# Sign bit by VectorE, a direct split of weights, pooling placed by the plan, and a plan that scores by age of readiness

## The chip, the cores and the metric

The kernel runs on one core of a Trainium2 chip. The metric is the device time of the whole program in microseconds. The engines are named as the profile names them: PE (matmul) with PEld (its weight loads), DVE (VectorE), ACT (ScalarE), POOL (GpSimd) and SP (which here only issues DMAs). Each engine has its own queue and executes it in order: an instruction whose input isn't there yet holds everything behind it on that engine.

## What is computed

Three layers over 4608 tokens of 512 features. The inputs `q`, `k`, `v` are float32; the four weights and the gain `g_ln` arrive as float64, which on the chip are pairs of 32-bit words, a low word and a high word.

```python
k_p = k.reshape(B, H, 72, 8, 64).mean(axis=3)        # pooling by 8, the same for v
attn = softmax(q @ k_p.T / 8);  x = attn @ v_p        # 8 batches, 8 heads, 576 queries, 72 keys
h = x @ w_in                                          # 512 -> 1024
solu = h * softmax(h)
ln = (solu - mean) / sqrt(var + 1e-6) * g_ln
y = ln @ w_out                                        # 1024 -> 512
h = y @ w2_in                                         # 512 -> 2048
out = (h * sigmoid(1.702 * h)) @ w2_out               # 2048 -> 512
```

## The kernel before

**Two stages.** The first stage does attention and the first two-layer block, tile by tile (36 tiles of 128 tokens, in 18 pairs), and beside it turns `w2_in` and `w2_out` into what the second stage multiplies with. The second stage runs 12 blocks of 384 tokens through `w2_in` and `w2_out` in a seven-product scheme; its order is written out by hand and no line of it is touched here.

**Numbers in two halves.** A float32 value is held as two float16 values, `hi` and `lo`, and a product is three matmul passes. `lo` is the value minus `hi`.

**From float64 to float32.** A piece of 512 columns of a weight (tile `raw`) is joined from its words: ACT writes the sign (`sg`), ACT shifts the low word down, ACT scales the high word (this drops the exponent's excess), DVE (`scalar_tensor_tensor`, shift and or) puts the two together into the low word's place, and POOL multiplies by `sg`. For the first layer `joined` (L646 on) does it; for the second layer `values_of` (L590 on), whose POOL product goes to the tile `w_f`.

**Split of the first layer's weights.** `first_half` (L645 on) handles the 16 pieces of `w_in` and `w_out`: ACT scales the joined piece into `val` (float32, two buffers that it shares with `w_f`), ACT rounds `val` to `hi`, and a subtraction on POOL or DVE (`VG`, the plan's choice) makes `lo`.

**The second layer's weights.** `Quarter.run` takes the 16 chunks of 1024 columns, each two pieces through `values_of`, four sums of slots (`combine`), `hi` on ACT and `lo` by `VG`, and two DMAs to a scratch in HBM.

**Attention of a tile** (`attention(t)`): load `qt`; matmul `psx` (one buffer); on DVE the largest `mx` and the difference `e`; ACT exp; DVE sum `rs`; the product `e<-e,rs` by `VG`; ACT and `VG` split into `st`; an SP transpose `aT<-st`; matmul `psv` (one buffer); ACT and DVE evict it as `xT` (hi and lo). **Hidden layer** (`Pair.hidden`): 24 matmuls into `psh` (two buffers), DVE `hmx` and `nm`, ACT exp `he`, DVE `tt` with the mean, ACT squares. **Norm and projection**: small POOL operations, ACT `tt` and `zs`, `zs` lo by `VG`, an SP transpose `zT`, 96 matmuls into `psy` (one buffer, two rounds), ACT `y`, store.

**Pooling** (`half`, L758 on): keys and values of a batch are loaded in two halves each (`half`, three buffers), 32 in all. A half is summed by one DVE `tensor_reduce`, or by three POOL adds (`total`). Before, the dictionary `KV_POOL` sends two of the 32 to POOL: keys of batch 0, second half, and values of batch 1, second half.

**What sets the order.** The first stage is emitted by a planner that runs on the host as the kernel is built (`Plan`, L171 on). Each step of work is a generator (a strand) that offers its next operation. `estimate` gives an operation a start time in a model of the engines: the later of the engine's free time and of the operation's inputs being ready; an operation with a choice of engines (`VG`) takes the one where it ends first, with 3000 ns held against DVE. `run` then emits the strand with the least score, which is that time plus up to 900 ns either way for how far its tile's due time lies from now (doubled in the first 60 us of the model). So the model's time, and not what happens on the chip, fixes the order of every queue; `there(...)` is an entry for no engine, with which a strand waits in the model's time until a tile is there.

Of the kernel before, what the change touches and what calls it, by code (L numbers as in the profile page):

```python
# [18 lines left out]
P = 128  # L19
# [18 lines left out]
UW = 256  # L38
# [30 lines left out]
DUE_MAX_IN = -10000  # L69
DUE_MAX_OUT = 20000  # L70

RAWS = 4
SG = 4
TTS = 4
V_TOP = 2.0 ** 14

TOP3 = 2.0 ** -29 * (1 - 2.0 ** -23)
A_TOP = 2.0 ** 14
LN_UP = 2.0 ** 10
CI_LEAST, CI_MOST = 2.0 ** -50, 2.0 ** 40  # L80
# [91 lines left out]
class Plan:  # L172
# [30 lines left out]
    def drop(self, *tiles):  # L203
        for t in tiles:
            del self.ring_of[t.name]
# [12 lines left out]
    def estimate(self, op):  # L218
        best = None
        for engine in op.engines:  # L220
            t = max(self.free[engine], self.ready(op, engine))
            if engine == "sp":
                t = max(t, self.free["dma"] - 2000)
            if engine == "dve" and op.port and self.pool_from <= t < self.free["pool"]:
                t = self.free["pool"]
            key = t + op.cost[engine] + self.spare[engine] if len(op.engines) > 1 else t
            if best is None or key < best[0]:
                best = (key, t, engine)
        return best[1:]

    def take(self, op, t, engine):
# [25 lines left out]
    def run(self):  # L257
        while self.strands:
            self.strands.sort(key=lambda s: s.due)
            while any([s.settle() for s in self.strands]):  # L260
                self.strands = [s for s in self.strands if not s.ended]
            best = None
            for s in self.strands:
                if isinstance(s.item, Op):
                    t, engine = self.estimate(s.item)
                    slack = (s.due - (t if self.now is None else self.now)) * self.haste
                    score = t + max(-self.pull, min(self.pull, slack)) * (self.early if t < self.until else 1)
                    if best is None or score < best[0]:
                        best = (score, t, engine, s)
            if best is None:  # L270
                assert not self.strands, "strands wait for each other"
                break
            _, t, engine, s = best
            s.item.emit(engine)
            self.take(s.item, t, engine)
            s.advance(None)
            self.strands = [s for s in self.strands if not s.ended]
# [3 lines left out]
def moe_kernel(ctx: ExitStack, tc: tile.TileContext, qT, kT, vT, w_in, w_out, g_ln, w2_in, w2_out, eye, outT):  # L281
# [135 lines left out]
    with ExitStack() as ph:  # L417
# [75 lines left out]
        def G(name, *args, **kw):  # L493
            return op(("pool",), name, args, kw)

        def VG(name, *args, **kw):
            return op(("pool", "dve"), name, args, kw)

        def A(**kw):
            return op(("act",), "activation", (), kw)  # L500
# [89 lines left out]
        def values_of(raw, up, dst, begun=None):  # L590

            hw, lw = raw[:, :, 1], raw[:, :, 0]
            sg = yield New(kv, [P, WC], F16, "sg", bufs=SG)
            if begun is not None:
                begun.append(sg)
            yield A(out=sg, in_=hw.bitcast(F32), func=AF.Sign)
            yield A(out=lw.bitcast(U32), in_=lw.bitcast(U32), func=AF.Copy, scale=TOP3, bias=-0.49999)
            yield lambda: (up.name, up.offset) in upped
            yield A(out=hw.bitcast(F32), in_=hw.bitcast(F32), func=AF.Copy, scale=up)
            yield V(  # L600
                "scalar_tensor_tensor", out=lw, in0=hw, scalar=3, in1=lw, op0=ALU.logical_shift_left,
                op1=ALU.bitwise_or,
            )
            d = yield from dst()
            yield G("tensor_tensor", out=d, in0=sg, in1=lw.bitcast(F32), op=ALU.mult)
            drop(sg)

        def raw_new(q, n):
            return New(kv, [P, q, n, 2], I32, "raw", "raw", RAWS)
# [35 lines left out]
        def first_half(raw, measured, scaled, up, k, c, his):  # L645

            yield from joined(raw, measured)
            yield scaled
            val = yield New(kv, [P, NS, UW], F32, "val", "w_f", 2)
            v = val.rearrange("p s f -> p (s f)")[:, :WC]  # L650
            hi, lo = (x[:, k, c] for x in his)
            yield A(out=v, in_=raw[:, :, 0].bitcast(F32), func=AF.Copy, scale=up)
            yield A(out=hi, in_=v, func=AF.Copy)
            yield VG("tensor_tensor", out=lo, in0=v, in1=hi, op=ALU.subtract)
            drop(val)

        def halves(n):
            return [slice(j * WC, (j + 1) * WC) for j in range(n // WC)]
# [73 lines left out]
            scaled = start(scale(), due)  # L732
            yield until(*[start(part(i), due + 4 * i) for i in range(n)])

        KV_POOL = {("k", 0): 1, ("v", 1): 1}

        def spans(t):

# [19 lines left out]
        def half(kind, b, j, src, dst):  # L758

            raw = yield New(kv, [P, 2, SP, NPOOL], F32, "half", bufs=3)  # L760
            begun[kind][b] += 1
            yield D(raw.rearrange("p a s o -> p a (s o)"), src[b][:, 2 * j : 2 * j + 2])
            yield from total(G if KV_POOL.get((kind, b)) == j else V, dst[:, 2 * j : 2 * j + 2], raw)
            drop(raw)

        def pooled(kind, b, src, due):
# [413 lines left out]
        def eye_load():  # L1180
            yield D(eye_t, eye)

        plan.early, plan.until = PULL_EARLY, EARLY_END
        plan.pull, plan.haste, plan.spare = PULL, HASTE, {"pool": 0.0, "dve": SPARE}

# [294 lines left out]
```

## Time and profile before

| | us |
|---|---|
| Median of three runs (lowest, highest) | 1255.61 (1253.86, 1258.69) |
| The profiled execution | 1253.29 |
| its span, first to last instruction | 1251.5 |
| PE busy | 1143.5 (91%) |
| DVE busy | 730.9 (58%) |
| ACT busy | 766.5 (61%) |
| POOL busy | 664.7 (53%) |

The profiled execution has 1.8 us around its span and lies 2.3 us under the median. The page gives shares over the whole span; since the two stages have different limits, the rows that follow are taken by stretches. A row of a group of instructions shows its line, engine and operation, output and inputs by name, shapes and number, then the total busy time and the mean length of one in ns, then the engine's idle time just before these instructions and what ended it. Line 475 and line 512 are the helpers through which the planner emits everything, so the names of the tiles tell the instructions apart.

### The profile page before, as it was taken

To read this page: it belongs to the slowest core of one execution; us is meant where nothing else is said; L and a number is where in the kernel's file an instruction comes from. 1 tells how busy PE (TensorE), PEld (TensorE's weight loads), DVE (VectorE), ACT (ScalarE), POOL (GpSimd) and SP (SyncE) were. 2 spreads that over 40 slices of the span, in tenths; PEclk is the share of its full clock that TensorE was granted. 3 is DMA by queue.
4 is the path that set the end of the run, shared out by engine and by line. 5 is a ranking of instruction groups with operands and counts; after the bars stand their busy time and mean duration, and the time that the engine had idled before them with its cause. 6 is when DMAs were issued, how large, how long until landed. Compare 5 with 4: busy or idle time off the path is not lost.

```text
span 1251.5 us, 27586 instructions
## 1 busy us (share of the span) xinstructions
PE 1143.5 (91%) x11678; PEld 989.6 (79%) x11678; DVE 730.9 (58%) x1153; ACT 766.5 (61%) x1073; POOL 664.7 (53%) x696
## 2 busy tenths in 40 slices
PE   2778998899999999889999999999999999999998
PEld 2335665576666666789999999999999898999998
DVE  7898877587677843136455454637272737364543
ACT  6998998788789855345445353627263536454552
POOL 5887998687879953424333352525262515243331
PEclk9989999899999999999999999999999999999999
DMA  9979999999989698470101010100011010101000
GB/s 324 302 205 240 269 270 256 248 231 248 256 206 234 164 230 236 109 270 8 46 14 39 14 40 20 33 27 27 27 33 46 7 46 8 46 7 46 14 14 26
DMA packets 246524, 152.85 MB, mean 122 GB/s; under 512 B 163584, under 2 KB 226176, under 8 KB 244096
## 3 DMA queue, kind: packets, MB, share of 16 engines
q1 hardware_dynamic: 246400, 151.09, 45.5%
q8 instruction: 91, 1.49, 0.5%
q14 instruction: 33, 0.27, 0.1%
HBM read 77.66 MB, written 33.55 MB: 89 GB/s over the span
## 4 chain that ended last, share of the span: by engine, by line
PE 30%; POOL 12%; DVE 8%; ACT 8%; issue 5%; DMA 0%; ACTq 0%; POOLq 0%
PE bank_a L1290 18%; PE bank_d L1290 8%; ACT w_g L1325 6%; DVE g L1337 5%; POOL w_g L336 3%; PE bank_b L1290 3%; POOL w_g L335 3%; POOL w_g L333 2%; POOL w_g L334 2%; PE psy L512 2%; ACT g L1334 1%; DVE c L1303 1%; POOL zs L475 1%; DVE w_g L333 0%; ACT c L1300 0%
## 5 line engine op out<-in xcount | busy, mean ns | idle before, releaser
L1290 PEld LDWEIGHTS <-w2i 128*128 128x128 f16 x4032 | 337.4, 98 | 34.3 <-issue 33.7
L1290 PEld LDWEIGHTS <-w2o 128*128 128x128 f16 x4032 | 335.0, 98 | 7.4 <-issue 6.8
L333 POOL TENSOR_TENSOR w_g<-w_g 128x384 f32<-128x384 f32 x36 | 43.6, 1211 | 379.3 <-ACT w_g L1325 379.3
L1290 PE MATMUL bank_a<-ys,w2i 128*128 128x192 f16 x2304 | 215.1, 247 | 27.1 <-ACT c L1300 25.0
L512 PE MATMUL psh<-w1i,xT 128*128 128x512 f16 x864 | 205.8, 389 | 8.9 <-DVE mean L475 8.2
L1290 PE MATMUL bank_a<-g,w2o 128*128 128x192 f16 x2304 | 206.0, 246 | 1.0
L512 PE MATMUL psy<-zT,w1o 128*128 128x256 f16 x1728 | 196.8, 273 | 8.8 <-ACT y L475 8.8
L512 PEld LDWEIGHTS <-w1o 128*128 128x128 f16 x1728 | 167.9, 98 | 35.8 <-issue 10.3
L1337 DVE SCALAR_TENSOR_TENSOR g<-w_g,gu_b,g 128x1152 f16<-128x1152 f32 (+1 forms) x96 | 169.1, 1782 | 24.5 <-ACT g L1334 24.4
L512 PEld LDWEIGHTS <-xT 128*128 128x128 f16 x864 | 84.4, 100 | 103.9 <-issue 13.8
L1300 ACT ACTIVATE c<-bank_a 128x384 f32<-128x384 f32 x192 | 91.7, 484 | 116.4 <-PE bank_a L1290 113.1
L1334 ACT ACTIVATE g<-w_g,gu_b 128x1152 f16<-128x1152 f32 (+1 forms) x96 | 132.9, 1408 | 39.4 <-POOL w_g L336 39.0
L1303 DVE SCALAR_TENSOR_TENSOR c<-bank_d,c 128x384 f32<-128x384 f32 x96 | 53.3, 555 | 134.4 <-ACT c L1300 99.5
L475 POOL TENSOR_TENSOR zs<-tt,zs 128x1024 f16<-128x1024 f32 x36 | 77.4, 2149 | 59.7 <-ACT zs L475 59.5
L1290 PE MATMUL bank_d<-ys,w2i 128*128 128x192 f16 x1152 | 107.5, 249 | 0.3 <-DVE c L1303 0.3
L1290 PE MATMUL bank_d<-g,w2o 128*128 128x192 f16 x1152 | 102.4, 246 | 3.0 <-DVE g L1337 3.0
L1325 ACT ACTIVATE w_g<-c,ch_b 128x1536 f32<-128x1536 f32 x48 | 75.3, 1568 | 36.8 <-DVE c L1303 36.7
L1300 ACT ACTIVATE c<-bank_a,co_b 128x384 f32<-128x384 f32 x47 | 26.9, 573 | 108.6 <-PE bank_a L1290 108.6
L512 PE MATMUL psx<-kbd,qt 128*128 128x144 f32 (+1 forms) x320 | 46.3, 306 | 24.6 <-ACT raw_z L475 12.7
L512 PEld LDWEIGHTS psx<-kbd,qt 128*128 128x128 f32 (+1 forms) x320 | 41.4, 193 | 29.4 <-issue 12.7
L475 POOL TENSOR_TENSOR lo<-w_f,hi 128x512 f16<-128x512 f32 (+1 forms) x46 | 62.2, 1365 | 2.7 <-ACT hi L475 2.3
L475 DVE TENSOR_REDUCE hmx<-psh 128x1 f32<-128x1024 f32 x36 | 43.7, 1214 | 34.1 <-PE psh L512 34.1
(189 smaller groups left out, 1693.1 us busy)
## 6 DMA issues: line engine op xcount, KB each, us to landing
raw<-w_out SPq DMA_DIRECT2D x12, 1024.0 KB, 6.9
raw<-w_in SPq DMA_DIRECT2D x10, 1024.0 KB, 8.0
half<-kT SPq DMA_DIRECT2D x16, 576.0 KB, 5.4
half<-vT SPq DMA_DIRECT2D x16, 576.0 KB, 5.5
qt<-qT SPq DMA_DIRECT2D x36, 256.0 KB, 3.9
y_dram<-y SPq DMA_DIRECT2D x36, 256.0 KB, 2.8
y<-y_dram SPq DMA_DIRECT2D x48, 192.0 KB, 3.2
outT<-c SPq DMA_DIRECT2D x48, 192.0 KB, 1.9
```

The source lines that it names most:

```text
L333: eng.tensor_tensor(out=w[:, 1], in0=q[:, Q12], in1=q[:, Q11], op=ALU.subtract)
L334: eng.tensor_tensor(out=w[:, 2], in0=q[:, Q22], in1=w[:, 1], op=ALU.subtract)
L335: eng.tensor_tensor(out=w[:, 0], in0=q[:, Q22], in1=q[:, Q12], op=ALU.subtract)
L336: eng.tensor_tensor(out=w[:, 3], in0=q[:, Q21], in1=w[:, 2], op=ALU.subtract)
L475: getattr(eng, name)(*args, **kw)
L512: nc.tensor.matmul(*p[:3], start=p[3], stop=p[4])
L1290: nc.tensor.matmul(bank[:, q], self.weight(p, q, kk, w), self.data(p, kk, i), start=(first and q == 0 and kk == 0 and w == 0 and i == 0), ...
L1300: nc.scalar.activation(out=self.c[:, i], in_=bank, func=AF.Copy, scale=self.scale)
L1303: nc.vector.scalar_tensor_tensor(out=self.c[:, i], in0=bank, scalar=self.scale, in1=self.c[:, i], op0=ALU.mult, op1=ALU.add)
L1325: nc.scalar.activation(out=self.w[:, 0:4], in_=self.c, func=AF.Gelu_apprx_sigmoid, scale=self.ch)
L1334: nc.scalar.activation(out=self.g[:, 0, s], in_=self.w[:, s], func=AF.Copy, scale=self.gu)
L1337: nc.vector.scalar_tensor_tensor(out=self.g[:, 1, s], in0=self.w[:, s], scalar=self.gu, in1=self.g[:, 0, s], op0=ALU.mult, op1=ALU.subtract,)
```

## The change

- `values_of`: the ACT sign and the POOL product go. After the shift-and-or, a second DVE `scalar_tensor_tensor` takes the sign bit of the scaled high word and ors it onto the joined word, straight into `w_f`. `joined`, the first layer's form, stays as it is.
- `first_half`: no `val`. ACT makes `hi` straight from the joined piece with the scale, and a DVE `scalar_tensor_tensor` makes `lo` as piece times scale minus `hi`.
- `half`: a `there(raw)` ahead of the sum, then the choice: batch 0 as before; from batch 1 on POOL takes a half where the model has POOL free more than 1300 ns before DVE.
- `Plan`: the score is no longer made from the start time but from the later of the start time and the inputs' readiness plus 700 ns (nothing is added for `there`).

```diff
+POOL_MORE = 1300
+MARGIN = 700
+SIGN = -(2 ** 31)
@@ Plan.estimate
-            t = max(self.free[engine], self.ready(op, engine))
+            there = self.ready(op, engine)
+            t = max(self.free[engine], there)
...
-                best = (key, t, engine)
+                best = (key, t, engine, max(t, there + self.margin[engine]))
@@ Plan.run
-                    t, engine = self.estimate(s.item)
+                    t, engine, safe = self.estimate(s.item)
...
-                    score = t + max(-self.pull, min(self.pull, slack)) * (self.early if t < self.until else 1)
+                    score = safe + max(-self.pull, min(self.pull, slack)) * (self.early if t < self.until else 1)
@@ values_of
-            sg = yield New(kv, [P, WC], F16, "sg", bufs=SG)
-                begun.append(sg)
-            yield A(out=sg, in_=hw.bitcast(F32), func=AF.Sign)
+                begun.append(True)
...
-            yield G("tensor_tensor", out=d, in0=sg, in1=lw.bitcast(F32), op=ALU.mult)
-            drop(sg)
+            yield V(
+                "scalar_tensor_tensor", out=d.bitcast(I32), in0=hw, scalar=SIGN, in1=lw, op0=ALU.bitwise_and,
+                op1=ALU.bitwise_or,
+            )
@@ first_half
-            val = yield New(kv, [P, NS, UW], F32, "val", "w_f", 2)
-            v = val.rearrange("p s f -> p (s f)")[:, :WC]
             hi, lo = (x[:, k, c] for x in his)
-            yield A(out=v, in_=raw[:, :, 0].bitcast(F32), func=AF.Copy, scale=up)
-            yield A(out=hi, in_=v, func=AF.Copy)
-            yield VG("tensor_tensor", out=lo, in0=v, in1=hi, op=ALU.subtract)
-            drop(val)
+            v = raw[:, :, 0].bitcast(F32)
+            yield A(out=hi, in_=v, func=AF.Copy, scale=up)
+            yield V("scalar_tensor_tensor", out=lo, in0=v, scalar=up, in1=hi, op0=ALU.mult, op1=ALU.subtract)
@@ half
-        KV_POOL = {("k", 0): 1, ("v", 1): 1}
+        KV_POOL = {("k", 0): 1}
...
-            yield from total(G if KV_POOL.get((kind, b)) == j else V, dst[:, 2 * j : 2 * j + 2], raw)
+            yield there(raw)
+            free = plan.free["pool"] + POOL_MORE < plan.free["dve"]
+            yield from total(G if (b == 0 and KV_POOL.get((kind, b)) == j) or (b and free) else V, dst[:, 2 * j : 2 * j + 2], raw)
@@ where the plan's settings stand
+        plan.margin = dict.fromkeys(plan.free, MARGIN)
+        plan.margin["none"] = 0
```

## Rows read from the trace of the kernel before

**Rows 1.** The page: busy tenths of each engine in 40 slices of 31.3 us.

```profile
PE   2778998899999999889999999999999999999998
DVE  7898877587677843136455454637272737364543
ACT  6998998788789855345445353627263536454552
POOL 5887998687879953424333352525262515243331
```

**Rows 2.** Windows: stretch, length, busy of PE, PEld, DVE, ACT, POOL; clock, DMA share, GB/s.

```profile
0.00:36.00 36.00, 10.60 (x52) 9.65 (x53) 29.11 (x51) 26.49 (x46) 21.04 (x29) 1.00 0.95 323
36.00:120.00 84.00, 64.64 (x444) 35.87 (x444) 73.38 (x144) 76.35 (x129) 66.81 (x79) 0.90 0.95 243
120.00:220.00 100.00, 92.27 (x747) 63.40 (x747) 78.47 (x138) 91.77 (x147) 92.27 (x112) 1.00 1.08 267
220.00:460.00 240.00, 225.41 (x1807) 155.62 (x1805) 171.33 (x324) 195.58 (x306) 198.80 (x259) 0.99 0.93 227
560.00:1251.00 691.00, 660.57 (x7840) 650.79 (x7837) 352.16 (x457) 333.09 (x393) 255.82 (x184) 1.00 0.09 27
```

**Rows 3.** Waits of PE from 36 to 520 us: total, times, longest.

```profile
PE psv L512 <- DVE xT L475: 10.3, 5, 5.2
PE psv L512 <- DMA aT<-st: 9.4, 3, 7.3
PE psh L512 <- DVE mean L475: 8.2, 4, 3.7
PE psy L512 <- ACT y L475: 8.0, 4, 3.0
```

**Rows 4.** Timeline of PE and DVE: start, length, instruction, [idle before <- releaser].

```profile
36.19 3.80 PE L512 MATMUL psh<-w1i,xT 128*128 128x512 f16 x12
...
64.08 2.75 PE L512 MATMUL psh<-w1i,xT 128*128 128x512 f16 x12
...
77.14 1.07 PE L512 MATMUL psv<-aT,vst 128*64 128x128 f16 x16 [7.31 <-DMA aT<-st]
...
242.67 1.35 DVE L475 TENSOR_REDUCE kp<-half 128x144 f32<-128x1152 f32 x1 [5.77 <-DMA half<-kT]
...
245.81 0.80 PE L512 MATMUL psv<-diag,ones 128*128 128x128 f32 x2 [5.21 <-DVE xT L475]
...
246.40 4.50 PE L512 MATMUL psh<-w1i,xT 128*128 128x512 f16 x12
```

**Rows 5.** Groups of instructions, 0 to 560 us: what the change takes away.

```profile
L475 ACT ACTIVATE sg<-raw 128x512 f16<-128x512 f32 x44 | 29.1, 661 | 0.0
L475 POOL TENSOR_TENSOR w_f<-sg,raw 128x512 f32<-128x512 f16 x32 | 41.1, 1294 | 2.9 <-DVE raw L475 2.8
L475 ACT ACTIVATE w1i<-val 128x512 f16<-128x512 f32 x8 | 4.8, 626 | 0.1
L475 POOL TENSOR_TENSOR w1i<-val,w1i 128x512 f16<-128x512 f32 x8 | 10.0, 1266 | 0.2 <-ACT w1i L475 0.2
L475 POOL TENSOR_TENSOR w1o<-val,w1o 128x512 f16<-128x512 f32 x8 | 9.6, 1212 | 0.5 <-ACT w1o L475 0.5
```

**Rows 6.** The same view: nearest kin of what is added or moved; last, one tile's min/median/max.

```profile
L475 DVE SCALAR_TENSOR_TENSOR raw<-raw 128x512 int32<-128x512 int32 x44 | 41.6, 959 | 0.9 <-ACT raw L475 0.8
L475 DVE SCALAR_TENSOR_TENSOR xT<-psv,xT 128x512 f16<-128x512 f32 x36 | 24.7, 685 | 5.2 <-ACT xT L475 5.0
L475 DVE TENSOR_REDUCE kp<-half 128x144 f32<-128x1152 f32 x15 | 20.1, 1339 | 9.6 <-DMA half<-kT 9.6
L475 POOL TENSOR_TENSOR half<-half 128x576 f32<-128x576 f32 x2 | 2.8, 1410 | 2.6 <-DMA half<-kT 2.6
L475 DVE TENSOR_TENSOR e<-e,rs 128x576 f32<-128x576 f32 x8 | 12.5, 1563 | 0.0
L475 DVE SCALAR_TENSOR_TENSOR raw<-raw x44: 634/743/2366, 26.5 to 424.8; 128x512 int32<-128x512 int32 x44
```

## The prediction

> **What bounds the kernel now.** I read the busy tenths first, to find the stages, then windows by stage, then what PE waited for, then single places in the timeline, and last the groups of instructions that the diff names.
>
> The tenths show two stages [rows 1]. Up to slice 13 DVE, ACT and POOL are mostly at 7 to 9 tenths, like PE; the first stage ends in slice 17 (some 540 us), and from there PE alone is full. In the second stage PE is busy 660.6 of 691 us [rows 2], and the diff touches no line of it. So the change can act only on the first stage, and there only on the time that PE doesn't use. By windows [rows 2], PE leaves 25.4 us of the first 36 (its first hidden-layer product starts at 36.19 [rows 4]), 19.4 of the next 84, 7.7 of the next 100 and 14.6 of the 240 up to 460. Past 220 us PE is busy 94% of the time: it is the bound, and work taken off ACT or POOL there buys nothing by itself. What can be won is the start, the PE idle time up to 460 us, and the time lost at a lower granted clock.
>
> The waits [rows 3] say what ends PE's idle time from 36 to 520 us: DVE's eviction `xT` 10.3 us, the transposes `aT` 9.4, DVE's `mean` (which frees `psh`) 8.2, ACT's `y` 8.0; 36 us together. They are few and long. The timeline shows the making of two [rows 4]. At 242.67 a pooling sum stands at the head of DVE and has waited 5.77 us for its load; `xT` is behind it, and PE stands 5.21 us. After that idle time the clock is down: the next 12 `psh` products take 4.50 us, where 12 at full clock take 2.75, so 1.75 us more. At 77.14 PE has waited 7.31 us for `aT`, in the stretch whose mean granted clock is 0.90 [rows 2, 4]. These stalls come from an order fixed in the planner's model, which a late transfer doesn't change.
>
> **The change part by part.**
>
> *Split of the first layer, 16 pieces.* Of three operations two stay: `val` becomes the new `hi`, so ACT loses 16 x 0.626 = 10.0 us [rows 5]. POOL loses 10.0 + 9.6 = 19.6 us [rows 5]. DVE gains 16 `scalar_tensor_tensor` of 512 columns. No row has this form; its nearest are 0.685 us (one input in PSUM, float16 out) and 0.959 (the mean of both in SBUF, with a longest of 2.366) [rows 6], so 11.0 to 15.3 us, and since both inputs lie in SBUF I take 15.3.
>
> *Sign bit, 32 pieces.* ACT loses 32 x 0.661 = 21.2 us, POOL 41.1 [rows 5]; DVE gains 32 x 0.685 to 0.959 = 21.9 to 30.7, and I take 30.7, for the same reason [rows 6]. The chain of a piece gets shorter, by 1.294 against 0.959 and the step between two engines, but nobody on the path of a tile waits for it: it feeds the second stage's weights, done by about 460 us.
>
> Together ACT loses 31, POOL 61, DVE gains 46 (33 at the lower end).
>
> *Pooling by the plan.* One of the 28 halves from batch 1 on was on POOL; each further one that goes there takes 1.34 us from DVE [rows 6] and gives POOL three adds, the first of 1.41 us, the others with a half and a quarter of its elements, some 2.5 us (an estimate). POOL is 61 us lighter, so I take 10 moved: DVE -13, POOL +25. The eight `e<-e,rs` on DVE, 12.5 us [rows 6], stand there because the model found POOL late; with POOL freer most go back: DVE -12 at most. DVE ends 46 - 13 - 12 = 21 us heavier, with 0 to 46 as bounds, against the 10.6 + 21.5 + 68.7 = 101 us that it leaves free from 36 to 460 [rows 2]. POOL ends some 25 lighter, ACT 31.
>
> *No effect of their own.* `there(raw)` is emitted to no engine; the real wait of the sum for its load stays, on whichever queue it goes to. The sums that go to POOL no longer hold DVE; behind them on POOL stand `st`, `e` and `zs`, so a late load then delays `aT` or `zT` by the same time instead of `xT`. SP gets no new DMA and loses none.
>
> *The margin.* An operation is put off by up to 700 ns in favour of others whose inputs have been there for longer. What is emitted isn't changed, only the order, on all queues, SP's among them: transposes that wait for a `zs` or a `st` just made go behind loads that are ready. On each queue it costs a chain at most 0.7 us a step where other work is ready, and nothing where the engine is behind. For it speaks that most waits of PE are for steps that came later than the model thought. Its price can't be read from the trace: the bounds are nothing, and all four kinds of rows 3.
>
> **Sum.** Start: up to 36.19 the pieces of `w_in` run on ACT, DVE and POOL; with one ACT operation of 0.626 less for each of the first four pieces and no POOL subtraction behind them, 2 to 3 us; the added DVE work takes some of it back, as DVE is busy 29 of the first 36 [rows 2]. I take -2 (bounds -4 and +3). From 36 to 460: of the 36 us of rows 3, those for `xT` and `aT`, 19.7, are long stalls of the kind that a different age order and moved sums break up; I take half, -10. The clock comes back with the stalls: one such place is 1.75 us [rows 4], two of them -3. For `mean` and `y`, 16.2 together, ACT's relief and DVE's load go against each other: nothing. New stalls from an order that is dealt anew: +3, the size of one of the shorter `mean` waits [rows 3]. Sum -2 - 10 - 3 + 3 = -12, on the profiled execution's own 1253.3: 1241.3. That execution lies 2.3 under the median of 1255.6; the comparison would be with the latter, and I leave the number at 1241.
>
> **The rivals.**
>
> *Same (1249 to 1259).* PE's idle time is what is left between long chains that share single buffers (`psx`, `psv`, `psy`), and a new order only deals it out elsewhere. For it: past 120 us PE is busy 92 to 94% [rows 2], and the relief falls on ACT and POOL, which end only 8 of the 36 us of waits of rows 3 (`y`). Against it: the stalls have single, long causes. It gives -2 at the start and nothing else: 1251.
>
> *Slower: DVE ends last on the tile's chain.* From 36 to 120 us DVE is busy 73.4 of 84 us, and nearly all 16 new `lo` fall in there: 73.4 + 11.0 to 15.3 = 84.4 to 88.7, over the whole window. It decides from the point where fewer than four of the pooling sums of that stretch (4 x 1.34 = 5.4) go to POOL. Then `mean` and `xT`, which already end 18.5 us of PE's waits, come later by up to the overrun of 4.7 us, and as these are in-order queues the later sign instructions stand ahead of them too: 32 x 0.959 = 30.7, of which I let one third reach PE, 10. That gives 1253.3 + 5 + 10 - 3 = 1265.
>
> The rows show such lengthening: the same DVE form takes 0.634 us at the least and 2.366 at the most, with a mean of 0.959 [rows 6]. The Trainium skill speaks for this rival and against the change: by "SBUF — State Buffer", section "Who interferes with whom", a VectorE instruction with two inputs in SBUF shares a read port with GpSimd, and whichever comes second stands until the other has ended; all 48 new instructions are of this kind. The row agrees in direction; by the rule taken to its end each would wait out a POOL operation of about 1.2 us, and the sum's DVE gain would be near 90 us instead of 46.
>
> *More (1222 to 1233).* All of the waits for `xT` and `aT` (19.7) go, the clock is back (5), and the start gives 4, with no new stall: 1253.3 - 29 = 1224.
>
> *It doesn't do what it says.* POOL's model time may hardly ever lie 1300 ns under DVE's, so that no sum moves; this is the condition of the slower rival, and counted there.
>
> **How the numbers follow.** The forecast (1233 to 1249) has 0.50, same 0.22, more 0.14, slower 0.14. Half a per cent, 6.3 us, is about what a measurement of this kernel can tell from no change. Faster by more than that: 0.50 + 0.14 = 0.64; within it 0.22; slower 0.14. The range runs from 1227, which leaves out the lower part of the gain without any new stall, to 1262, which leaves out most of the slower case: about 2 in 10 outside.
>
> **What would show it.** In the changed kernel's trace: no `val`, 16 `sg` left, 48 more `scalar_tensor_tensor` on DVE with means between 0.69 and 0.96; ACT of the first 460 us lower by about 30 and POOL's by about 25; some ten pooling sums on POOL. If the forecast holds, the rows "PE psv <- DVE xT" and "PE psv <- DMA aT" together halve, and the first stage ends some 12 us earlier, with the second as long as before. If DVE is the new bound, its window from 36 to 120 us is full and "PE psh <- DVE mean" grows. I would be wrong if the first hidden-layer product starts later than 36 us, if the end of the first stage is moved by its tail rather than by these waits, or if the second stage's length changes.

## The result: slower by one per cent

The changed kernel takes 1269.18 us (median of four runs, 1266.71 to 1272.02), the kernel before 1255.42 beside it: a ratio of 1.0103, 95% interval 1.0074 to 1.0131. The profiled execution takes 1269.69 us with a span of 1267.9, 16.4 us more than before. PE's 11678 matmuls are the same. The time parts at the last product of the first stage, which ends at 536 us before and at 558.2 here (columns as in [rows 2], the first two lines from before):

```profile
0.00:536.00 536.00, 462.36 (x3616) 318.87 (x3617) 370.37 (x686) 422.06 (x666) 403.81 (x508) 0.98 0.92 235
536.00:1251.50 715.50, 681.10 (x8062) 670.74 (x8061) 360.55 (x467) 344.41 (x408) 260.86 (x188) 0.99 0.11 38
0.00:558.20 558.20, 472.50 (x3616) 324.54 (x3617) 385.63 (x724) 396.22 (x631) 369.22 (x474) 0.97 0.91 226
558.20:1268.00 709.80, 676.89 (x8062) 666.56 (x8061) 360.01 (x467) 344.30 (x408) 260.39 (x188) 1.00 0.11 38
```

The first stage is 22.2 us longer: PE is idle 12.1 us more, and the same products hold it 10.1 us longer, at a granted clock of 0.97 after 0.98. What follows, the second stage, is 5.7 us shorter, 4.2 of it in PE's products (granted clock 1.00 after 0.99); in the profiled executions of the eighteen kernels below it takes 708.8 to 714.7 us, with no edit in it, so that little can be read into this.

The windows of the changed kernel:

```profile
0.00:36.00 36.00, 10.54 (x36) 8.89 (x37) 29.23 (x48) 22.50 (x40) 20.95 (x24) 1.00 0.96 314
36.00:120.00 84.00, 60.05 (x408) 34.68 (x408) 75.87 (x154) 68.48 (x120) 50.39 (x72) 0.90 0.89 230
120.00:220.00 100.00, 89.64 (x703) 60.32 (x702) 66.57 (x121) 70.87 (x113) 62.32 (x84) 0.97 1.04 229
220.00:460.00 240.00, 221.96 (x1745) 153.23 (x1744) 182.86 (x351) 186.33 (x298) 196.60 (x238) 0.97 0.94 226
```

Against [rows 2], PE is busy 4.6 us less in the second window, 2.6 less in the third, 3.5 less in the fourth: the loss lies all over the first stage. ACT and POOL have become emptier, as forecast (ACT is 26.0 us less busy over the span, POOL 35.1), and PE got nothing for it.

The waits of PE from 36 to 520 us, which answer to [rows 3]:

```profile
PE psv L516 <- DVE xT L479: 11.0, 6, 2.6
PE psh L516 <- DVE mean L479: 10.2, 5, 4.1
PE psv L516 <- DMA aT<-st: 9.4, 3, 4.9
PE psv L516 <- DMA vst<-vx: 8.7, 4, 3.4
PE psv L516 <- ACT diag L479: 4.2, 3, 2.3
PE psy L516 <- DMA zT<-zs: 4.1, 1, 4.1
PE psv L516 <- DVE rs L479: 3.9, 1, 3.9
```

`xT` and `aT` together are 20.4 us, where they were 19.7 and were to halve. `mean` has grown from 8.2 to 10.2, and the loads of values (`vst`) from 3.5 to 8.7; `diag` on `psv`, `zT` and `rs` stand where no such rows stood before. Of the four rows of [rows 3] only `y` fell, from 8.0 to 1.6. Summed over all rows by what ended them, waits for DVE grew from 22.5 to 25.6 us, for ACT they fell from 9.8 to 9.2, and for DMA they grew from 12.9 to 23.7: most of what is new in this window ends with a load or a transpose. What made those late was not followed.

The groups of the first 565 us, which answer to [rows 5, 6]:

```profile
L479 DVE SCALAR_TENSOR_TENSOR raw<-raw 128x512 int32<-128x512 int32 x44 | 35.2, 824 | 0.1
L479 DVE SCALAR_TENSOR_TENSOR w_f<-raw 128x512 int32<-128x512 int32 x32 | 27.7, 888 | 0.7 <-POOL lo L479 0.7
L479 DVE SCALAR_TENSOR_TENSOR w1o<-raw,w1o_gs,w1o 128x512 f16<-128x512 f32 x8 | 5.5, 737 | 0.0
L479 DVE SCALAR_TENSOR_TENSOR w1i<-raw_z,w1i_up,w1i 128x512 f16<-128x512 f32 x4 | 3.1, 800 | 0.0
L479 DVE SCALAR_TENSOR_TENSOR w1i<-raw,w1i_up,w1i 128x512 f16<-128x512 f32 x4 | 2.8, 738 | 0.0
L479 POOL TENSOR_TENSOR half<-half 128x576 f32<-128x576 f32 x5 | 7.0, 1406 | 11.5 <-DMA half<-kT 11.5
L479 POOL TENSOR_TENSOR e<-e,rs 128x576 f32<-128x576 f32 x35 | 41.0, 1172 | 26.8 <-DVE rs L479 25.9 <-DVE nm L479 0.7
```

The 48 new DVE instructions take 27.7 + 5.5 + 3.1 + 2.8 = 39.1 us. Five halves are summed on POOL, three more than before; `e<-e,rs` went back to POOL, seven of the eight.

Two places of the timeline show short DVE steps that come late. The first is the making of `w_in`'s scale, a chain of short DVE steps (start, length, instruction):

```profile
29.00 0.28 DVE L479 TENSOR_REDUCE w1i_all<-psy 128x1 f32<-128x128 f32 x1
...
29.30 1.07 DVE L479 SCALAR_TENSOR_TENSOR raw<-raw 128x512 int32<-128x512 int32 x1
30.30 0.14 DVE L479 TENSOR_SCALAR w1i_all<-w1i_all 128x1 f32<-128x1 f32 x1
...
31.92 1.33 DVE L479 TENSOR_REDUCE vp<-half 128x144 f32<-128x1152 f32 x1
33.17 0.20 DVE L479 TENSOR_SCALAR rc<-rc 128x1 f32<-128x1 f32 x1
33.30 1.33 DVE L479 TENSOR_REDUCE kp<-half 128x144 f32<-128x1152 f32 x1
...
35.34 0.20 DVE L479 TENSOR_SCALAR w1i_up<-rc 128x1 f32<-128x1 f32 x1
```

From `w1i_all` to `w1i_up` it takes 6.3 us; before, the steps stood back to back and took 1.4 us (27.43 to 28.83). Each step becomes ready only when the one before it ends, so with the margin something older goes ahead of it each time, and is then waited out whole, 1.33 us in two cases. PE's first hidden-layer product starts at 44.13 us instead of 36.19. The second place is where the new `lo` of `w_out` stand:

```profile
82.10 1.21 DVE L479 TENSOR_REDUCE hmx<-psh 128x1 f32<-128x1024 f32 x1
83.23 0.74 DVE L479 SCALAR_TENSOR_TENSOR w1o<-raw,w1o_gs,w1o 128x512 f16<-128x512 f32 x1
83.89 0.68 DVE L479 SCALAR_TENSOR_TENSOR xT<-psv,xT 128x512 f16<-128x512 f32 x1
84.49 3.38 DVE L479 SCALAR_TENSOR_TENSOR w1o<-raw,w1o_gs,w1o 128x512 f16<-128x512 f32 x5
87.80 0.20 DVE L479 TENSOR_SCALAR nm<-hmx,h_sc 128x1 f32<-128x1 f32 x1
...
88.58 0.67 DVE L479 SCALAR_TENSOR_TENSOR xT<-psv,xT 128x512 f16<-128x512 f32 x1
```

`nm`, which opens the way from `hmx` to the next use of `psh`, had its inputs when `hmx` ended at 83.31, and stands behind six pieces of a weight, 4.1 us, and an `xT`; the next `xT` is behind it.

### The profile page after: what moved, and what is told of

It is laid out like the page before. It is cut to its first block, busy times and chain, and to the rows that moved or that the text cites. A ratio compares the mean times of both kernels' runs of the same rounds, so it can differ in the third digit from the quotient of the medians.

```text
span 1267.9 us, 27577 instructions
## 1 busy us (share of the span) xinstructions
PE 1149.4 (91%) x11678; PEld 991.1 (78%) x11678; DVE 745.6 (59%) x1191; ACT 740.5 (58%) x1039; POOL 629.6 (50%) x662
## 3 DMA queue, kind: packets, MB, share of 16 engines
q1 hardware_dynamic: 246400, 151.09, 46.1%
## 4 chain that ended last, share of the span: by engine, by line
PE 41%; DVE 18%; POOL 14%; ACT 11%; DMA 8%; issue 7%; SPq 1%; ACTq 0%; POOLq 0%; DVEq 0%
PE bank_a L1296 17%; PE psy L516 7%; PE bank_d L1296 7%; DVE g L1343 6%; ACT w_g L1331 6%; PE psh L516 6%; POOL w_g L340 3%; POOL w_g L339 3%; POOL w_g L337 2%; DMA raw<-w_in 2%; POOL w_g L338 2%; DMA raw<-w_out 2%; PE bank_b L1296 2%; PE psx L516 1%; ACT g L1340 1%
## 5 line engine op out<-in xcount | busy, mean ns | idle before, releaser
L516 PE MATMUL psh<-w1i,xT 128*128 128x512 f16 x864 | 210.7, 395 | 10.2 <-DVE mean L479 10.2
L516 PE MATMUL psy<-zT,w1o 128*128 128x256 f16 x1728 | 201.1, 275 | 9.0 <-DMA zT<-zs 6.2
L516 PEld LDWEIGHTS <-w1o 128*128 128x128 f16 x1728 | 170.5, 99 | 40.9 <-issue 6.7
L1296 PE MATMUL bank_d<-ys,w2i 128*128 128x192 f16 x1152 | 104.8, 246 | 0.3 <-DVE c L1309 0.3
L1309 DVE SCALAR_TENSOR_TENSOR c<-bank_b,c 128x384 f32<-128x384 f32 x48 | 26.7, 555 | 65.5 <-ACT c L1306 48.7
```

Of the source, the lines that this page charges most:

```text
L516: nc.tensor.matmul(*p[:3], start=p[3], stop=p[4])
L1296: nc.tensor.matmul(bank[:, q], self.weight(p, q, kk, w), self.data(p, kk, i), start=(first and q == 0 and kk == 0 and w == 0 and i == 0), ...
L1309: nc.vector.scalar_tensor_tensor(out=self.c[:, i], in0=bank, scalar=self.scale, in1=self.c[:, i], op0=ALU.mult, op1=ALU.add)
```

## The experiments

Four theories. **A, the margin:** it puts DVE's short chains off, and that is the loss. **B, DVE's load:** the 48 instructions stand ahead of the tiles' steps on a queue that was full at the start. **C, a picked order:** the settings of the kernel before fit its order, and any new order is worse. **D, the plan:** what is asked of the planner (other operations, the pooling's choice, the margin) gives a worse order by itself. All ratios are medians against the kernel before, run beside each kernel (its median lay between 1255.2 and 1257.3 us), with 95% intervals. Spans, busy times and traces are those of one profiled execution, and single executions of one kernel lie up to 9 us from its median, so differences of a few us between two traces tell nothing by themselves. In the recorded expectations of the sign bit, the split, the relief and the load, D, D' and E name other theories, each explained where it is named.

### The margin taken away, alone, and not for DVE

Four kernels: the changed one with `MARGIN = 0`; the one before with the margin and nothing else; the changed one without margin and with the old pooling (the two weight edits alone); and the changed one with the margin on all engines but DVE.

```diff
-        plan.margin["none"] = 0
+        plan.margin["none"] = plan.margin["dve"] = 0
```

Margin 0: 

> The changed kernel with the margin set to 0 ns; sign bit, direct split and pooling by the plan stay. Theory A (the margin puts DVE's short chains of just-ready steps behind other work): the scale of w_in is known near 29 us again instead of 36.9, the first hidden-layer product starts near 35 us instead of 44, and the time comes out at 1241 to 1255. Theory B (the 48 added DVE instructions overfill DVE, as in the rival of the prediction): still 1264 or more, the first product at 40 us or later. Theory C (any new order deals PE's idle time anew): anywhere from 1245 to 1270, without the start telling which.

Margin alone: 

> The kernel before with the margin of 700 ns alone. Theory A: slower than before, 1265 to 1275, with the scale of w_in late by 5 us or more and the first hidden-layer product at 41 us or later. Theory B: 1250 to 1258, no slower than before, since nothing is added to DVE. Theory C: anywhere from 1245 to 1270.

Weights alone: 

> Sign bit and direct split alone: no margin, pooling as before. Theory A: 1241 to 1252, and about 5 above the kernel with margin 0 if moving sums to POOL helps. Theory B: slower than the kernel with margin 0, since no sum leaves DVE: 1265 or more, DVE from 36 to 120 us at 80 of 84 us or more. Theory C: 1245 to 1270.

Margin, not on DVE: 

> The changed kernel with the margin 0 for DVE and 700 ns for the other queues. Theory A: the scale chain is on DVE, so most of the loss goes: 1245 to 1258, the first hidden-layer product before 38 us. Theory B: no help, 1264 or more. Theory C: 1245 to 1270.

| kernel | us | ratio |
|---|---|---|
| margin 0 | 1272.09 | 1.0104 [1.0059, 1.0150] |
| margin alone | 1263.38 | 1.0054 [1.0029, 1.0080] |
| weights alone, by the plan | 1268.51 | 1.0097 [1.0067, 1.0126] |
| margin, not on DVE | 1270.52 | 1.0093 [1.0066, 1.0119] |

Without the margin the changed kernel is as slow as with it, and the two weight edits alone bring all of it. These two are one finding, not two: by their traces, both kernels have the same operations in the same order on every queue, since without the margin the pooling's choice sends no more sums to POOL than before (two of 32). So the margin isn't needed for the loss, and A falls as its cause. That the margin puts the start off is shown: with the margin alone the first hidden-layer product starts at 46.12 us, with the margin on all engines but DVE in the changed kernel at 36.05, and that kernel is as slow all the same. B named a first product at 40 us or later for margin 0; it starts at 32.29. The margin alone costs half a per cent, between what A (1265 or more) and B (1258 at most) gave. The timeline of PE with margin 0 shows why the start alone doesn't decide:

```profile
32.29 2.74 PE L516 MATMUL psh<-w1i,xT 128*128 128x512 f16 x6 [0.69 <-ACT xT L479]
...
36.30 1.46 PE L516 MATMUL psh<-w1i,xT 128*128 128x512 f16 x6
...
44.74 5.08 PE L516 MATMUL psh<-w1i,xT 128*128 128x512 f16 x12 [0.70 <-ACT xT L479]
```

The first hidden product starts at 32.29, four us ahead of [rows 4], but its 24 matmuls end at 49.8; before, they ended at 45.0. The waits for `xT` from 36 to 520 us are nearly three times those of [rows 3]:

```profile
PE psv L516 <- DVE xT L479: 28.5, 10, 8.5
```

### The new instructions in the old order, and other orders of the old ones

To part the instructions from the order, the planner was shown the operations of the kernel before, and what was emitted for each was the new instruction or nothing. The queues of PE and SP are then line for line those of before (the traces agree: the same 11678 products and 352 DMAs in the same order).

```diff
@@ first_half (values_of alike)
-            yield A(out=v, in_=raw[:, :, 0].bitcast(F32), func=AF.Copy, scale=up)
-            yield A(out=hi, in_=v, func=AF.Copy)
-            yield VG("tensor_tensor", out=lo, in0=v, in1=hi, op=ALU.subtract)
+            x = raw[:, :, 0].bitcast(F32)
+            yield emitted(A(out=v, in_=x, func=AF.Copy, scale=up), nothing)
+            yield emitted(A(out=hi, in_=v, func=AF.Copy), lambda engine: nc.scalar.activation(out=hi, in_=x, func=AF.Copy, scale=up))
+            yield emitted(
+                VG("tensor_tensor", out=lo, in0=v, in1=hi, op=ALU.subtract),
+                lambda engine: nc.vector.scalar_tensor_tensor(out=lo, in0=x, scalar=up, in1=hi, op0=ALU.mult, op1=ALU.subtract),
+            )
```

Three kernels do the reverse: the instructions of before, with one setting of the planner moved a little (`HASTE = 0.0101`; `SPARE = 2950`; PE's delay in `LAG` 199 instead of 197), which deals the order anew.

Both edits, old order: 

> The new instructions of sign bit and direct split in the order of the kernel before: the planner plans the old operations, and what is emitted in their places is the new ones (ACT's sign and val: nothing; POOL's product and lo: the DVE instruction). PE's and SP's queues are then line for line those of before. Theory B (48 more DVE instructions delay the tiles): 1264 or more, with the wait of psv for xT well above before's 10 us. Theory C (the new deal of the order is what costs, not the instructions): 1246 to 1257.

Old instructions, new orders: 

> The kernel before with HASTE 0.0101 instead of 0.01: the same instructions, a slightly new order. Theory B: no change beyond noise, 1252 to 1259. Theory C: a new order alone costs, because the kernel before sits at a lucky one: 1259 to 1270.

 

> The kernel before with SPARE 2950 instead of 3000: a second small new order, about as many places changed as by HASTE. Theory B: 1252 to 1259. Theory C: 1259 to 1270.

 

> The kernel before with 199 instead of 197 ns after PE in the planner's model: a third new order, with some three times as many places of PE's queue changed. Theory B: 1252 to 1259. Theory C: 1259 to 1272, and no less than the two smaller ones.

| kernel | us | ratio |
|---|---|---|
| both edits, old order | 1266.37 | 1.0066 [1.0042, 1.0089] |
| before, `HASTE` 0.0101 | 1255.24 | 0.9993 [0.9969, 1.0017] |
| before, `SPARE` 2950 | 1251.35 | 0.9961 [0.9937, 0.9985] |
| before, `LAG` of PE 199 | 1251.26 | 0.9946 [0.9922, 0.9970] |

C falls for small changes of the order: none of the three is worse than before, and two are better, just under the 1252 that B gave as its lowest. B holds for the time: with no line of PE's or SP's queue moved, the instructions alone cost 0.66%, two thirds of the loss. B's sign in the trace does not hold: `xT` was to end well over 10 us of PE's waits and ends 10.3, as before; what grew is `mean` (8.2 to 12.2), with 2.8 for `w1i`. So the long `xT` waits of margin 0 come with the new order, and not with the instructions alone.

### Which of the two edits, and load or relief

In the old order again: the sign bit alone; the split alone; the relief alone (nothing added to DVE; signs of the second layer left out, with the shift-and-or at the place of the product, and `lo` of the first layer set to nothing by 16 short POOL instructions); and the load alone (all work of before, and 48 DVE instructions of the new forms into a tile that nobody reads).

```diff
@@ first_half of the load alone (values_of alike)
-            yield VG("tensor_tensor", out=lo, in0=v, in1=hi, op=ALU.subtract)
+            def both(engine):
+                eng = {"dve": nc.vector, "pool": nc.gpsimd}[engine]
+                eng.tensor_tensor(out=lo, in0=v, in1=hi, op=ALU.subtract)
+                nc.vector.scalar_tensor_tensor(out=extra, in0=v, scalar=up, in1=hi, op0=ALU.mult, op1=ALU.subtract)
+
+            yield emitted(VG("tensor_tensor", out=lo, in0=v, in1=hi, op=ALU.subtract), both)
```

Sign bit: 

> Sign bit alone, in the order of the kernel before (32 DVE instructions come, 32 signs on ACT and 32 products on POOL go). Theory B (the added DVE time costs, ACT's and POOL's relief returns little): 1260 to 1264, its share of the 9 us by the later rise of the delay over the tiles (from about 8 at tile 9 to 13). Theory D (the start costs it all): 1255 to 1259.

Split: 

> Direct split alone, in the order of before (16 DVE instructions, all before 95 us). Theory B: 1260 to 1265, since PE was delayed by 7.7 us by tile 9 with both edits and only this one acts there. Theory D': a delay at the start is caught up later, 1255 to 1259.

Relief: 

> Relief without load, order of before: the signs of the second layer's weights are left out (so its output has them positive), the lo halves of the first layer's weights are set to zero by 16 short POOL memsets instead of being computed, and nothing is added to DVE. Theory B: at or a little below before, 1249 to 1257; the relief of ACT and POOL buys less than 8 us. Theory E (it is the missing instructions' place in the order, not DVE's time): slower than before, 1260 or more, like with the DVE instructions.

Load: 

> Load without relief, order of before: nothing is taken away, and the same 48 DVE instructions are added at the same places with their results thrown away. Theory B: the full price of the load, 1264 to 1276, more than with the relief (1266). Theory E: near before, 1253 to 1260.

| kernel, old order | us | ratio | DVE busy, against before | span |
|---|---|---|---|---|
| sign bit | 1256.85 | 1.0006 [0.9991, 1.0021] | +15.0 | +2.8 |
| split | 1264.58 | 1.0071 [1.0046, 1.0096] | +10.8 | +9.1 |
| both edits | 1266.37 | 1.0066 [1.0042, 1.0089] | +22.5 | +9.7 |
| relief alone | 1252.48 | 0.9976 [0.9955, 0.9998] | -11.9 | +3.2 |
| load alone | 1278.74 | 1.0180 [1.0161, 1.0200] | +46.1 | +24.2 |

The relief of ACT and POOL is worth a quarter of a per cent (0.45% at most, by the interval); the load on DVE costs 1.8%, more than was expected (1276 at most), with 48 instructions that take 53.9 us there, beside all of POOL's old work, where the changed kernel's take 39.1. And it isn't the amount alone that counts: the sign bit puts more on DVE than the split and costs nothing that can be measured (0.2% at most, by the interval), where 1260 to 1264 us were expected if DVE's time as such cost. The two edits differ in place: the sign's instructions start between 123 and 446 us, where PE is busy 93% of the time, the split's between 31 and 97. DVE in the split kernel (start, length, instruction; no idle time between):

```profile
31.00 0.74 DVE L667 SCALAR_TENSOR_TENSOR w1i<-raw_z,w1i_up,w1i 128x512 f16<-128x512 f32 x1
31.66 0.68 DVE L475 SCALAR_TENSOR_TENSOR raw<-raw 128x512 int32<-128x512 int32 x1
32.27 0.75 DVE L475 TENSOR_TENSOR e<-psx,mx 128x576 f32<-128x576 f32 x1
32.93 1.10 DVE L667 SCALAR_TENSOR_TENSOR w1i<-raw_z,w1i_up,w1i 128x512 f16<-128x512 f32 x1
33.96 1.34 DVE L475 TENSOR_REDUCE vp<-half 128x144 f32<-128x1152 f32 x1
35.22 0.68 DVE L475 SCALAR_TENSOR_TENSOR xT<-psv,xT 128x512 f16<-128x512 f32 x1
```

`xT` of the first tile starts at 35.22 instead of 33.51, pushed by 0.74 + 1.10 of the two new instructions ahead of it. Then PE, which begins the first tile's product in time, runs out of `lo` of `w_in` three times:

```profile
36.07 2.56 PE L512 MATMUL psh<-w1i,xT 128*128 128x512 f16 x9
39.79 0.81 PE L512 MATMUL psh<-w1i,xT 128*128 128x512 f16 x3 [1.15 <-DVE w1i L667]
...
43.47 0.38 PE L512 MATMUL psh<-w1i,xT 128*128 128x512 f16 x1 [1.74 <-DVE w1i L667]
45.04 1.44 PE L512 MATMUL psh<-w1i,xT 128*128 128x512 f16 x3 [1.19 <-DVE w1i L667]
```

Before, POOL's `lo` ended one such wait, of 0.58 us. These waits are in part hidden: the first tile's product ends 5.2 us late, but the third tile's begins 2.7 late (62.24 after 59.53), since it waited for DVE's `mean` before, too. The delay of `hmx`, which follows a tile's hidden product, grows from 3.0 us at the first tile to 9.4 at the sixth (some 109 us) and is 11.7 at the last: what is lost in the first 110 us is not caught up behind it, where PE is busy 93 to 95% of the time. First to last `hmx`, before and with the split:

```profile
L475 DVE TENSOR_REDUCE hmx<-psh x36: 1168/1215/1226, 52.6 to 495.5; 128x1 f32<-128x1024 f32 x36
L475 DVE TENSOR_REDUCE hmx<-psh x36: 1167/1216/1230, 55.6 to 507.2; 128x1 f32<-128x1024 f32 x36
```

Some of that delay is chance: the relief, by its median no slower than before, shows 2.8 us at the sixth tile and 4.4 at the last, the sign bit 1.8 and 6.2. What sets the split apart is the delay by the sixth tile; its price is the median's 0.71%.

The split does one thing more. With `val` gone, a piece in `raw` (four buffers) is held until DVE's `lo` has read it, and the next load into that buffer waits. SP's waits from 36 to 120 us, the first two with the split, the last before:

```profile
SPq L504 <- DVE w1o L667: 8.5, 2, 4.3
SPq L504 <- DVE w1i L667: 5.4, 1, 5.4
SPq L504 <- ACT val L475: 5.1, 3, 4.0
```

One load of `w2_in` that ACT's `val` released at 81.56 us is released by DVE's `w1o` at 91.15, and the next transpose `aT` stands behind it in SP's queue. How the 0.71% parts between steps behind the new instructions, PE's waits for `lo` and these loads was not tested.

### Each part by the plan, and wide new orders

One part of the change each, ordered by the planner: the sign bit, the split, the pooling (with its `there`), and the margin on all engines but DVE. Last, the instructions of before with wider changes of the settings: all delays of `LAG` longer (230, 180, 190, 95, 1150 ns), and the tiles' due times 12100 ns apart with `PULL = 820`. Counted in the emitted queues, these two move 7600 and 9300 lines of PE's queue; the sign bit by the plan moves 7100, the pooling 10350, the margin 9600.

```diff
-    LAG = {"pe": 197, "dve": 150, "act": 160, "pool": 75, "dma": 950}
+    LAG = {"pe": 230, "dve": 180, "act": 190, "pool": 95, "dma": 1150}
```

Sign bit by the plan: 

> Sign bit alone, planned by the planner (no margin, old split, old pooling). If the price of the weights part is the split's: 1252 to 1259, like with the order kept (1257). If the planner's new order is what makes the planned weights part dearer than the kept order: 1262 or more.

Split by the plan: 

> Direct split alone, planned by the planner. If DVE's load in the first 110 us is the cause: 1260 to 1268, as with the order kept (1264.6), since DVE is just as full. If the planner can make room for it: 1252 to 1259.

Pooling by the plan: 

> Pooling by the plan alone. With POOL as full as it was, the model's POOL is seldom 1300 ns ahead of DVE, so only a few of the 28 sums move: 1250 to 1260, no change that can be told. If it is worth something by itself: below 1250. If late loads now hold POOL: above 1262.

Margin but not on DVE, alone: 

> The margin alone on the kernel before, with DVE exempt. Theory A (the margin's loss is the scale chain and the other short DVE chains that it delays): 1251 to 1258, with the first hidden-layer product before 39 us. If the other queues carry the loss: 1261 to 1266, as with DVE included (1263).

Longer delays: 

> The kernel before with the model's delays between engines set longer (pe 230, dve 180, act 190, pool 95, dma 1150 ns instead of 197, 150, 160, 75, 950): the same operations, with an order dealt anew about as widely as in the planned kernels with one part of the change (on PE some 7600 lines of the queue stand elsewhere, where the sign bit alone by the plan moves some 7100, and DVE and SP as many as there). If an order dealt anew as widely costs by itself, whatever the operations are (the kernel before holds a picked order), this run is 4 to 9 us slower than before, ratio 1.003 to 1.007, as the pooling (1.0032) and the sign bit (1.0059) by the plan were. If what those two cost is due to what they ask of the planner, it stays within 3 us of before, as the three smaller changes of order did (0.9946 to 0.9993).

Due times: 

> The kernel before with the due times of the tiles 12100 ns apart instead of 12000, and 820 ns of pull instead of 900: the same operations, on PE some 9300 lines of the queue stand elsewhere, as many as with the margin alone (9600) or the pooling alone (10350). If a wide new order costs by itself: 4 to 9 us slower than before, ratio 1.003 to 1.007. If not: within 3 us of before.

| kernel | us | ratio |
|---|---|---|
| sign bit by the plan | 1261.41 | 1.0059 [1.0035, 1.0084] |
| split by the plan | 1265.26 | 1.0085 [1.0056, 1.0114] |
| pooling by the plan | 1258.8 | 1.0032 [1.0010, 1.0054] |
| margin alone, not on DVE | 1259.51 | 1.0032 [1.0012, 1.0051] |
| before, longer delays | 1246.22 | 0.9925 [0.9899, 0.9950] |
| before, due times 12100 | 1260.34 | 1.0046 [1.0021, 1.0071] |

The sign bit by the plan and the margin without DVE fall between the two cases that were named for each (1259 and 1262, 1258 and 1261). C falls for wide changes too: the longer delays were to be 4 to 9 us slower by it, or within 3 us without it, and are 10 us faster; the due times came out 3.5 slower. Of five new orders of the same instructions one is worse, one the same, three better, from 0.9925 to 1.0046. That is also how far a new order went by itself, up or down, and pooling (1.0032), margin (1.0054, or 1.0032 without DVE) and the sign bit's order (1.0059, against 1.0006 in the old one) lie at its upper end, with intervals that overlap the 1.0046. So D stays **open**: all four came out above 1, where three of five orders dealt without a purpose came out below, but a draw can't be told from a cause with so few. Only the split's price stands apart, since it shows with no line of PE's queue moved (1.0071, and 1.0085 by the plan). The pooling's choice alone leaves POOL with two sums, as before, one of them another, so what it costs is an order, and not moved work.

The best of all is the kernel before with longer delays in the model, 1246.22 us: faster than both kernels of this case. Its waits of PE from 36 to 520 us:

```profile
PE psv L512 <- DMA aT<-st: 16.0, 5, 7.7
PE psv L512 <- DVE xT L475: 8.3, 7, 3.1
PE psy L512 <- ACT y L475: 6.3, 3, 4.3
PE psh L512 <- DVE mean L475: 3.5, 4, 1.8
```

`aT` is longer than in [rows 3], `xT` and `mean` shorter. Yet in its profiled execution the first stage ends no earlier than before (536.2 us after 535.7); the 3.6 us of span that it gains there (it was the slowest of its runs) lie behind that, in the stage that no edit touches. Why this order does better was not followed further.

## Why the prediction was wrong

**The loads and reliefs: near.** Forty-eight instructions on DVE were put at 46 us, with bounds of 33 and 46, and take 39.1; their means, 0.737 to 0.888, lie between the forecast's 0.685 and 0.959. DVE ends 14.7 us heavier (forecast 21), ACT 26 lighter (31), POOL 35 (25). Seven of eight `e<-e,rs` went back.

**The step that failed: DVE's load set against its free time.** The text weighed DVE's 21 us against 101 us that DVE leaves free from 36 to 460 us, and let them cancel against ACT's relief, so that they cost nothing behind the start. Both edits' instructions in the old order cost 0.66% of the time, some 8 of the 13.8 us. A free share of a window says nothing of the place. The split's 14 us stand between 31 and 97 us, where DVE runs almost back to back, in one queue with `xT`, `nm` and `hmx`; PE waits for the `lo` of `w_in` itself, and loads wait for the pieces that `lo` reads. In the old order that costs 0.71% by itself. The sign bit, twice as many instructions, costs nothing that can be measured, as forecast: nobody on a tile's path waits for it, and PE is the bound there. Which of the two spares it wasn't tested. The rest of the loss, some 5 us, is within what a new order did by itself (up to 0.46%).

**The start: -2 forecast.** The gain was argued from shorter work on ACT and POOL; the added DVE work was mentioned and given bounds of -4 and +3. With the split alone the product starts in time (36.07), and the loss comes inside and behind it, some 3 us for the first tile and 9 by the sixth, outside the bounds. In the changed kernel the start is 8 us late (44.13, the sign that was named for an error), by the margin's handling of a chain of short steps: with DVE exempt it is 36.05. Yet with margin 0 the first product starts 4 us early and the kernel is as slow: the first product's start is a poor measure of the start.

**The waits for `xT` and `aT`: -10 forecast.** They went from 19.7 to 20.4 us. The forecast took a new order to break up long stalls. A new order deals them anew: in the five orders of the old instructions the time of the kernel went from -0.75 to +0.46%, so this term should have been nothing, with a width of 6 to 9 us to either side. The clock's -3, which hung on it, went the other way: the granted clock fell from 1.00 to 0.97 between 120 and 220 us and from 0.99 to 0.97 between 220 and 460. PE's products of the first stage take 10.1 us longer; how much of this is the clock was not parted. The first stage ends 22.2 us later, where 12 earlier were forecast, and the second is 5.7 us shorter, where no change was; the latter is within what that stage varies between executions.

**Pooling: 10 halves forecast, three more on POOL.** The rival's condition, fewer than four in the stretch of 36 to 120 us, was met: the three POOL sums there begin at 48.70, 64.70 and 102.47. Without the margin none is added.

**New stalls: +3 forecast.** The waits for `vst`, `diag`, `zT` and `rs` come to 21.8 us (0.9 of it `diag` on `psy`), where before `vst` was 3.5, `diag` 1.3 and the other two nothing: some 17 more. Against them stand 6.4 less for `y` and 4.5 less for three that no longer appear (`v_all`, `kbd`, `w2all`).

**The margin: no price, bounds from nothing to all waits.** These bounds let it work only for the good. The text named a cost ("at most 0.7 us a step") and didn't set it against the chain of seven short steps at the start, where it is paid at each. The 0.7 was too low, too: a step waits until the instruction put ahead of it has ended, up to 1.33 us. Alone it costs 0.54%, beside the others nothing that can be told.

**The rival "DVE ends last on the tile's chain"** gave 1265 and a chance of 0.14. In kind it is nearest to what the old order shows, where `mean` ends more of PE's waits (10.7 us with the split, 12.2 with both edits, 8.2 before) and the split's place decides. In the changed kernel itself `mean` and `xT` end only 2.7 us more. That its sum came near the measured time is luck. It let DVE's window from 36 to 120 us overflow to 84 or more; in the changed kernel it is 75.87 of 84, and the time is lost in single steps that come late. And it let a third of the sign bit's 30.7 us reach PE, where that edit costs nothing.

## What to carry to other kernels

Work moved to an engine costs what it delays at its place in the queue, not a share of the engine's free time: look for what stands behind it in the stretch where that engine runs back to back, whether somebody waits for the new result itself, and which buffer is now held until it is done. Where a planner orders the work, every edit also deals a new order; run several harmless changes of its settings first, to learn how far the time goes by that alone (here -0.75 to +0.46%), and emit the new instructions in the old order to see what they cost by themselves.

## What the runs showed of the chip

A DVE `scalar_tensor_tensor` of 512 columns from SBUF takes longer beside POOL. Of the 44 of the form raw<-raw in the kernel before, four ran with POOL idle (mean 0.683 us) and 21 with POOL busy throughout (mean 1.174); of the 76 int32 ones in the changed kernel (raw<-raw and w_f<-raw), 23 with POOL idle (0.683) and 28 beside it (1.004), 11 of these 28 in 0.673 to 0.693 us and the longest in 1.787. The same form as the sign's takes 0.844 us on the mean with the sign's POOL product gone, and 1.172 with it kept:

```profile
L617 DVE SCALAR_TENSOR_TENSOR extra<-raw 128x512 int32<-128x512 int32 x32 | 37.5, 1172 | 0.0
```

So taking work off POOL also makes DVE's own work shorter, and the relief and the load don't add up: 24.2 us of span for the load alone, 9.7 with the relief. The Trainium skill's "SBUF — State Buffer", section "Who interferes with whom", has a VectorE instruction with two inputs in SBUF share a port with GpSimd, as an exclusive lock: one waits until the other has ended. The runs agree in direction; the price seen is 0.3 to 0.5 us on the mean, from nothing in some instructions to 1.7 us in the longest (2.366 in the kernel before), and not the length of a POOL operation of 1.2 us in each.
